# Another order for the beginning of a packed-attention and gated feed-forward kernel

## The chip, the cores and the metric

The kernel runs on one core of a Trainium2 chip. Time is device time in microseconds (us), from an execution's start to its end; the runs before have a median of 695.22 us (three runs, 694.74 to 695.33).

## The reference

`x` is the result of an attention in two steps, and a gated feed-forward layer follows it:

```python
def _attn_ref(q, k, v, p):                       # q, k, v: 8 x 8 x 576 x 64; p: 8 x 8 x 32 x 64
    p_packed = sm_attn(p, k, v)                  # softmax(p k^T / 8) v
    return sm_attn(q, p_packed, p_packed)        # softmax(q p_packed^T / 8) p_packed

def _moe_ref(x, w_in, w_out):                    # x: 4608 x 512, w_in: 512 x 2048, w_out: 2048 x 512
    h = x @ w_in
    sp = np.maximum(h, 0.0) + np.log1p(np.exp(-np.abs(h)))
    return (h * erf(sp)) @ w_out
```

The weights come as 64-bit floats, so that a row of 512 of them is 4 KB.

## The kernel before, in words

The eight batches go one after the other, batches 0 and 1 in a beginning of their own. For a batch, `attention` computes the packed queries' scores against k, their softmax, and its product with v (the packed values); then the scores of q against the packed values and a second softmax, `second_softmax`, whose result is kept in two parts, `a2h` and `a2l` (a rounded value and the rest). The feed-forward layer never forms x: `w_prime` multiplies the packed values with a piece of w_in, the result is split into `wph` and `wpl` (`w_prime_high`, `w_prime_low`), and `h_half` multiplies these with a2: six products of 288 columns for 128 rows of h. Two such halves are a unit: unit n is half a batch's tokens (288) and 256 of the 2048 columns. `h_copy` brings them from PSUM to SBUF, `softplus`, `erf` and `gate` follow, and `o_part` multiplies with w_out.

For batch 0 the second softmax is split by token halves: N is the one of the first 288 tokens, X the one of the other 288. Units 0 to 3 (first half of the tokens) need N alone, units 4 to 7 need X.

Pieces of w_in: piece 0 (columns 0 to 511) is fetched in two halves, numbered 4 and 5 (256 columns each, 256 KB per chunk of 128 rows, four chunks); piece 1 is columns 512 to 1023 (512 KB per chunk). A fetched chunk is turned to 32 bits by a cast on ScalarE (line 121) and an operation on VectorE (line 125). Units 0 and 4 use half-piece 4, units 1 and 5 half-piece 5, and units 2, 3, 6, 7 piece 1.

The order of the beginning is written out by hand: `BEGINNING` is a list of words, each word calls one part, and `keep_order` makes every engine keep it. So what stands behind a word on its engine waits for it. The words that matter here: A and B are the next step of the attention of batch 0 and of batch 1; `F4.2` fetches chunk 2 of piece 4 on the SyncE (SP) queue, `F3` w_out's block 3; L and K are its cast and its operation; `W0.1`, `G0.1` (or H) and `V0.1` are w_prime of batch 0 and piece 1, its high and its low part; `h3.0` is the first half of unit 3, c and d copy it on ScalarE and VectorE; s, e and m are softplus, erf and gate; N and X are the next step of either half; `i11` is 11 products of the identity matrix with itself, whose result nobody uses.

The steps of batch 1 (`attention(1)`): its transfers of p and k; of v; of q; first scores (two words, each with a copy to SBUF behind it, lines 385 and 349); the maximum over them (line 427); two exponentials (452); six transposes of the result (402); their copy (460); four more transposes (407), and so on. At the end of the beginning's fourth line of words, at `h4.0`, both orders meet and are the same from there.

Of the kernel before, what the change touches and what calls it, by code (L numbers as in the profile page):

```python
# [8 lines left out]
F32 = mybir.dt.float32  # L9
F32R = mybir.dt.float32r  # L10
# [3 lines left out]
F16 = mybir.dt.float16  # L14
# [11 lines left out]
EXPONENT, TINY = 0x7F800000, 2.0 ** -55  # L26

BEGINNING = """
A A F4.2 F5.2 F4.3 A F5.3 F4.1 i11 A A i8 F5.1 F4.0 F5.0 A A A A F3 F1.2 B F1.3 F1.0 F1.1 A F2 A A A A A L5.2 L4.2 A A
A A A A L4.1 F0 F5 F1 N i21 B N N X L5.1 F7 N K4.1 K5.1 N L4.0 K5.2 K4.0 L4.3 N K4.3 K4.2 W0.4 N L5.0 K5.0 L5.3 N F4  # L30
H0.4 V0.4 K5.3 L3 N X i2 i1 i2 N X L1.2 W0.5 H0.5 V0.5 K1.2 B B B B B B L1.3 h1.0 c1.0 L1.0 K1.0 K1.3 L1.1 K1.1 X h1.1
F2.0 c1.1 h0.0 d0.0 X W0.1 G0.1 V0.1 L2 h0.1 h3.0 F6 X h3.1 d0.1 X X X X B B B s1 s0 e0 L0 F2.1 h2.0 h2.1 d2.1 c3.0
h4.0 h4.1 K0 L1 B d2.0 d3.1 e1 m0 h5.0 L5 B h5.1 d4.0 B c4.1 K1 o0.0 o0.2 K2 s3 d5.1 B L4 s2 s4 e4 S0 d5.0 o0.1 m1 K3
o1.2 T0 B B K5 o1.0 e3 K4 L7 m4 B L6 m3 K7 K6 h6.0 S1 o0.3 B c6.0 S4 R6 h6.1 T1 B B B c6.1 B S3 U4 o1.3 h7.0 e2 m2
h7.1 s5 o1.1 o2.1 o3.1 e5 B R2 B B o2.3 F2.3 d7.0 v4 T3 o2.0 F2.2 c7.1 L2.2 m5 T2 B B F3.2 L2.0 p3.1 o3.3 s6 p3.3 o2.2
# [15 lines left out]
def tile_pack_attention_moe(ctx: ExitStack, tc: tile.TileContext, qT, kT, v, pT, w_in, w_out, outT):  # L51
    nc = tc.nc
    P = 128
    B, _, NC, S = qT.shape
    DFF = w_in.shape[1]
    DM = w_out.shape[1]
    HT = S // 2
# [9 lines left out]
    NK = 32  # L67
# [3 lines left out]
    NB0 = 2  # L71
# [9 lines left out]
    apool = ctx.enter_context(tc.tile_pool(name="attn", bufs=2))  # L81
# [179 lines left out]
    a2 = {}  # L261
    pt = {}
    wp = {}
    halves = {}
# [15 lines left out]
    def second_softmax(b, ta, tb, mx, hi, lo, h0, h1, at=None, high=nc.scalar.copy):  # L280

        half = hi.dtype == F16

        cols = slice(h0, h1)
        blocks = ta[:, :, cols].rearrange("p r (n k) -> p r n k", k=NK)
        mx = mx[:, :, h0 // NK:h1 // NK]
        wide = mx.unsqueeze(3).to_broadcast([P, 2, (h1 - h0) // NK, NK])
        if at is not None:
            for r in range(2):
                nc.vector.transpose(ta[:, r, cols], at[r][:, 0:HT])  # L290
            yield
        nc.vector.tensor_reduce(mx, blocks, axis=AX.X, op=ALU.max)
        yield
        nc.vector.tensor_tensor(blocks, blocks, wide, op=ALU.subtract)
        yield
        nc.scalar.activation(ta[:, :, cols], ta[:, :, cols], AF.Exp, scale=SCALE)
        yield
        nc.vector.tensor_reduce(mx, blocks, axis=AX.X, op=ALU.add)
        yield
        if half:  # L300
            nc.vector.tensor_scalar(mx, mx, 1e-9, 2.0 ** -15, op0=ALU.add, op1=ALU.mult)
        else:
            nc.vector.tensor_scalar(mx, mx, 1e-9, None, op0=ALU.add)
        nc.vector.reciprocal(mx, mx)
        yield
        nc.vector.tensor_tensor(blocks, blocks, wide, op=ALU.mult)
        yield
        if h1 - h0 == S:
            nc.vector.transpose(tb[:].rearrange("p r s -> p (r s)"), ta[:].rearrange("p r s -> p (r s)"))
        else:  # L310
            for r in range(2):
                nc.vector.transpose(tb[:, r, cols], ta[:, r, cols])
        yield
        high(hi[:, :, cols], tb[:, :, cols])
        yield
        nc.vector.tensor_tensor(lo[:, :, cols], tb[:, :, cols], hi[:, :, cols], op=ALU.subtract)
        yield

    def attention(b):

        joined, third, roomy = b > NB0, b == NB0, b == 0
# [3 lines left out]
        def chunk(name, tag="kvq"):  # L325
            if tag == "kvq":
                return apool.tile([P, S], F32, name=f"{name}_{b}", tag="kvq", bufs=6)[:]
            if tag == "wo":
                return opool.tile([P, S], F32, name=f"{name}_{b}", tag="wo")[:]
            return tpool.tile([P, S], F32, name=f"{name}_{b}", tag=tag)[:]  # L330

        def bank(name, single=False):

            if single:
                return [ps_h.tile([P, 512], F32, name=f"{name}_{b}_{x}", tag="ps_h")[:] for x in range(2)], None
            if name in at_o:
                d = at_o[name]
                return [ps_o.tile([P, 512], F32, name=f"{name}_{b}_{x}", tag=f"ps_o{d + x}")[:] for x in range(2)], None
            ps = ps_m.tile([P, 2, 512], F32, name=f"{name}_{b}", tag="ps_m")
            return [ps[:, 0, :], ps[:, 1, :]], ps  # L340
# [19 lines left out]
        q_at = ("t0", "t0", "t0", "t1") if roomy else ("wo",) * NC if b == 1 else ("kvq",) * NC  # L360
        values, q = [], []

        def load_v():
            for j in range(NCH):
                n, t0 = (CH, j * CH) if j < NT else (REM, NT * CH + (j - NT) * REM)
                values.append(chunk(f"v{j}", v_at[j]))
                nc.sync.dma_start(values[j][0:n, 0:2 * NC * 64], v[b, t0:t0 + n, :])

        def load_q():
            for c in range(NC):  # L370
                q.append(chunk(f"q{c}", q_at[c]))
                nc.sync.dma_start(q[c], qT[b, :, c, :])

        if not joined:
            load_v()
            yield
            load_q()
            yield
        a1 = apool.tile([P, 2, S], F32, name=f"a1_{b}", tag="big", bufs=3)
        scores = []  # L380
        for c2 in range(2):
            banks = bank(f"s1_{c2}", joined or (third and c2 == 1))
# [67 lines left out]
        else:  # L450
# [20 lines left out]
            if joined:  # L471
                load_q()
# [24 lines left out]
            two_over(inverse[b][:], po[:, P:2 * P])  # L497
        yield
        ta = apool.tile([P, 2, S], F32, name=f"ta{b}", tag="big", bufs=3)
        for c2 in range(2):  # L500
            banks = bank(f"s2_{c2}", b > NB0 + 1 or (b >= NB0 and c2 == 0) or (b == 1 and c2 == 1))
            for c in range(NC):
                for r in range(2):
                    nc.tensor.matmul(banks[0][r][NK * c:NK * c + NK, 0:HT], ptt[64 * r:64 * r + 64, NK * c:NK * c + NK],  # L504
                                     q[c][64 * r:64 * r + 64, c2 * HT:(c2 + 1) * HT], start=True, stop=True)
            yield
            if roomy:
                scores.append(banks[0])
            else:
                for r in range(2):  # L510
                    nc.vector.transpose(ta[:, r, c2 * HT:(c2 + 1) * HT], banks[0][r][:, 0:HT])
                yield
        tb = apool.tile([P, 2, S], F32, name=f"tb{b}", tag="big", bufs=3)
        kind = F32R if b < NB0 else F16
        hi = apool.tile([P, 2, S], kind, name=f"a2h{b}", tag="a2h")
        lo = apool.tile([P, 2, S], kind, name=f"a2l{b}", tag="a2l")
        a2[b] = (hi, lo)
        mx = apool.tile([P, 2, S // NK], F32, name=f"mx{b}", tag="mx")
        if roomy:
            halves["N"] = second_softmax(b, ta, tb, mx, hi, lo, 0, HT, scores[2])  # L520
            halves["X"] = second_softmax(b, ta, tb, mx, hi, lo, HT, S, scores[3], nc.vector.tensor_copy)
            yield
            return
        every = second_softmax(b, ta, tb, mx, hi, lo, 0, S, None, nc.vector.tensor_copy if b < NB0 else nc.scalar.copy)
        for k, _ in enumerate(every):
            yield
# [242 lines left out]
    def attend(b):  # L769
        if b not in gens:  # L770
            gens[b] = attention(b)
        next(gens[b])
# [17 lines left out]
    f = 2  # L790
# [46 lines left out]
    def fetch(*which):  # L837
# [1 line left out]

    parts = {  # L840
        "A": lambda: attend(0), "B": lambda: attend(1), "C": lambda: attend(2),
        "N": lambda: next(halves["N"]), "X": lambda: next(halves["X"]),
        "F": fetch, "L": lambda *w: fetched[w][0](), "K": lambda *w: fetched[w][1](),
        "S": split_w_out_high, "T": split_w_out_low,
        "W": w_prime, "H": w_prime_high, "V": w_prime_low,
# [54 lines left out]
```

## Time and profile before

| | |
|---|---|
| runs | 694.74, 695.33, 695.22 us (median 695.22) |
| the profiled execution | 696.22 us, its span 694.4 us |
| TensorE (PE) busy | 679.4 us, 98% of the span |
| VectorE (DVE) busy | 600.4 us, 86% |
| ScalarE (ACT) busy | 556.2 us, 80% |
| GpSimd (POOL) busy | 53.7 us, 8% |
| DMA share by fortieth of the span, tenths | 9996456358351512211122301131021101000010 |

The span is cut into 40 slices of 17.4 us; the DMA engines are full in the first two and a half. A busy time counts PE's modelled ends, so small waits of PE are to be read from the list of waits and from the start times. A timeline row gives the start and the duration from the first to the last end in us, engine, line, operation, output and input with the number of records, and in brackets the idle time before it with what ended it. A 32-bit product counts as two records on PE.

### The profile page before, as it was taken

Reading aid. Unit: us, or ns where it says so; the run is one execution under the profiler, and the core shown is the slowest. Engines: PE = TensorE matmul, PEld = TensorE weight load, DVE = VectorE, ACT = ScalarE, POOL = GpSimd, SP = SyncE. Lnnn points to the kernel's source line nnn. Section 1 sums busy time; section 2 is a strip of 40 time slices with the busy share of each in tenths; the row PEclk is TensorE's granted clock in tenths of the full one; section 3 lists DMA queues with packets and bytes.
Section 4 is the critical chain, followed back from the end, with each engine's and each line's share of the span. In section 5 each row is a group of like instructions: output and inputs, shape, how many; then the busy total and the mean of one; then the engine's idle time right before and its main releaser. Section 6 shows DMA issues by size and latency. Waiting matters only on the chain.

```text
span 694.4 us, 15628 instructions
## 1 busy us (share of the span) xinstructions
PE 679.4 (98%) x6442; PEld 538.0 (77%) x6442; DVE 600.4 (86%) x937; ACT 556.2 (80%) x981; POOL 53.7 (8%) x80
## 2 busy tenths in 40 slices
PE   8999998999999999999999999999999999999997
PEld 6687988998888777867777776777777677777775
DVE  4999998889996999889988899798988899877775
ACT  2799977877778779887888888887898878787784
POOL 2031123102451000000000000000000000000000
PEclk9999999999999999999999999999999999999999
DMA  9996456358351512211122301131021101000010
GB/s 317 402 335 216 154 170 228 105 179 256 35 93 11 138 42 92 69 53 65 35 59 87 100 1 52 39 121 66 9 82 52 36 1 35 1 9 27 2 35 34
DMA packets 34311, 66.81 MB, mean 96 GB/s; under 512 B 4032, under 2 KB 13248, under 8 KB 34240
## 3 DMA queue, kind: packets, MB, share of 16 engines
q1 hardware_dynamic: 29600, 56.31, 24.4%
q0 software_dynamic: 4352, 8.92, 5.2%
q8 instruction: 50, 0.82, 0.5%
q10 hardware_dynamic: 288, 0.59, 0.2%
q14 instruction: 21, 0.17, 0.1%
HBM read 49.81 MB, written 15.99 MB: 95 GB/s over the span
## 4 chain that ended last, share of the span: by engine, by line
PE 62%; ACT 15%; DVE 13%; DMA 5%; issue 4%; POOL 1%; SPq 0%; ACTq 0%; POOLq 0%; DVEq 0%
PE o L637 35%; PE h L585 18%; PE wp L538 3%; DVE t L670 3%; DVE t L671 3%; ACT t L668 3%; ACT t L666 3%; ACT t L673 2%; ACT u L669 2%; DMA k<-kT 2%; DMA wi<-w_in 2%; DVE gl L620 2%; ACT ob L649 2%; PE p L414 1%; PE s L504 1%
## 5 line engine op out<-in xcount | busy, mean ns | idle before, releaser
L637 PE MATMUL o<-gh,woh 128*128 128x288 f16 x1536 | 304.5, 286 | 1.8 <-ACT ob L647 0.9
L637 PEld LDWEIGHTS <-woh 128*128 128x128 f16 x2304 | 223.4, 98 | 68.3 <-issue 12.8
L637 PE MATMUL o<-gl,woh 128*128 128x288 f16 x768 | 219.6, 286 | 0.5 <-DVE gl L620 0.4
L585 PE MATMUL h<-a2h,wph 128*128 128x288 f16 (+1 forms) x512 | 149.4, 292 | 4.2 <-ACT hs L593 2.8
L585 PE MATMUL h<-a2h,wpl 128*128 128x288 f16 (+1 forms) x512 | 147.7, 289 | 0.7 <-DVE wpl L562 0.7
L585 PE MATMUL h<-a2l,wph 128*128 128x288 f16 (+1 forms) x512 | 147.5, 288 | 0.0
L670 DVE SCALAR_TENSOR_TENSOR t<-hs,gs,t 128x576 f32<-128x576 f32 x96 | 78.3, 815 | 51.6 <-ACT u L669 50.9
L620 DVE TENSOR_TENSOR gl<-hs,gh 128x576 f16<-128x576 f32 (+1 forms) x124 | 96.3, 776 | 4.8 <-ACT gh L613 0.8
L673 ACT ACTIVATE t<-t 128x576 f32<-128x576 f32 x96 | 65.8, 686 | 41.6 <-DVE t L671 39.7
L637 PE MATMUL o<-gh,wohl 128*128 128x288 f32 x448 | 97.8, 299 | 0.0
L595 ACT ACTIVATE hs<-h 128x288 f32<-128x288 f32 x192 | 71.8, 407 | 30.5 <-PE h L585 28.5
L585 PEld LDWEIGHTS <-wph 128*128 128x128 f16 x768 | 74.9, 98 | 20.8 <-issue 1.8
L637 PEld LDWEIGHTS o<-gh,wohl 128*128 128x128 f32 x448 | 74.2, 188 | 6.4 <-issue 2.7
L671 DVE SCALAR_TENSOR_TENSOR t<-u,t 128x576 f32<-128x576 f32 x96 | 72.8, 758 | 3.3
L675 DVE SCALAR_TENSOR_TENSOR hs<-t,hs 128x576 f32<-128x576 f32 x96 | 71.9, 749 | 2.4 <-ACT t L673 2.4
L666 ACT ACTIVATE t<-hs,gs 128x576 f32<-128x576 f32 x96 | 73.7, 768 | 0.0
L668 ACT ACTIVATE t<-t 128x576 f32<-128x576 f32 x96 | 65.6, 684 | 3.0
L669 ACT ACTIVATE u<-t 128x576 f32<-128x576 f32 x96 | 65.6, 683 | 3.1
L637 PE MATMUL o<-gl,wohl 128*128 128x288 f32 x224 | 66.2, 295 | 0.0
L613 DVE CAST gh<-hs 128x576 f16<-128x576 f32 (+1 forms) x117 | 55.4, 474 | 4.3 <-PE o L637 4.0
L585 PEld LDWEIGHTS <-wpl 128*128 128x128 f16 x384 | 37.6, 98 | 9.5
L637 PEld LDWEIGHTS o<-gl,wohl 128*128 128x128 f32 x224 | 42.2, 188 | 0.1
(126 smaller groups left out, 824.4 us busy)
## 6 DMA issues: line engine op xcount, KB each, us to landing
q<-qT SPq DMA_DIRECT2D x32, 288.0 KB, 4.2
k<-kT SPq DMA_DIRECT2D x30, 288.0 KB, 5.2
wos<-w_out SPq DMA_DIRECT2D x16, 512.0 KB, 6.0
outT<-ob SPq DMA_DIRECT2D x48, 144.0 KB, 1.8
v<-v SPq DMA_DIRECT2D x24, 256.0 KB, 4.2
wi<-w_in SPq DMA_DIRECT2D x12, 512.0 KB, 6.9
outT<-ob POOLq DMA_DIRECT2D x32, 144.0 KB, 3.7
scratch<-wo POOLq DMA_DIRECT2D x16, 256.0 KB, 3.3
```

The source lines that it names most:

```text
L585: nc.tensor.matmul(ps[:, 0:HT], w[:, r, fo:fo + P], a[:, r, c * HT:(c + 1) * HT], start=(m == 0), stop=(m == 5))
L595: nc.scalar.mul(dst, src, 2.0 ** -19)
L613: copy(ghi[:], gs[n][0][:])
L620: nc.vector.tensor_tensor(glo[:], hs[:], ghi[:], op=ALU.subtract)
L637: nc.tensor.matmul(acc[b, c, d][:, 0:HT], w[f][:, d * P:(d + 1) * P], gg[:, k, :], start=(first and k == 0 and m == 0), stop=(last and k = ...
L666: nc.scalar.activation(t[:], hs[:], AF.Tanh, bias=T_BIAS, scale=scale[:, 0:1])
L668: nc.scalar.activation(t[:], t[:], AF.Square, bias=root * Q_BIAS, scale=root * Q_SCALE)
L669: nc.scalar.activation(u[:], t[:], AF.Tanh, bias=U_BIAS, scale=U_SCALE / A2)
L670: nc.vector.scalar_tensor_tensor(t[:], hs[:], scale[:, 1:2], t[:], op0=ALU.mult, op1=ALU.add)
L671: nc.vector.scalar_tensor_tensor(t[:], u[:], A1, t[:], op0=ALU.mult, op1=ALU.add)
L673: nc.scalar.activation(t[:], t[:], AF.Tanh, bias=A_BIAS, scale=A_SCALE)
L675: nc.vector.scalar_tensor_tensor(hs[:], t[:], 1.0, hs[:], op0=ALU.add, op1=ALU.mult)
```

## The change

The list of words is written anew up to `h4.0`, and two functions are cut so that it can be. (1) q of batch 0 is fetched in two column blocks per chunk (144 KB each instead of 288 KB), the second behind all of half-piece 5 (word Q). (2) The scores of its first block and N come first; the second block's scores are a step of their own behind `W0.4`. (3) Half-piece 4 is fetched before half-piece 5, and unit 0 is computed before unit 1. (4) Piece 1 of w_in is fetched before batch 1's p and k and before w_out's block 3. (5) Batch 1's first scores go behind units 0 and 1 on PE, and its maximum behind `V0.1` on VectorE. (6) Identity products: 11, 8, 13, 9, 3 and 6 instead of 11, 8, 21, 2, 1 and 2.

One line of the table, before and now:

```diff
-H0.4 V0.4 K5.3 L3 N X i2 i1 i2 N X L1.2 W0.5 H0.5 V0.5 K1.2 B B B B B B L1.3 h1.0 c1.0 L1.0 K1.0 K1.3 L1.1 K1.1 X h1.1
+K5.3 N h0.0 c0.0 h0.1 L1.3 c0.1 F4 K5.1 K5.0 W0.5 X X K1.2 H0.5 L1.0 V0.5 K1.3 L1.1 K1.0 B h1.0 c1.0 h1.1 c1.1 B B B B K1.1 X i3 W0.1
```

```diff
-        def load_q():
+        def load_q(c2=None):
             for c in range(NC):
-                q.append(chunk(f"q{c}", q_at[c]))
-                nc.sync.dma_start(q[c], qT[b, :, c, :])
+                if not c2:
+                    q.append(chunk(f"q{c}", q_at[c]))
+                cols = slice(0, S) if c2 is None else slice(c2 * HT, (c2 + 1) * HT)
+                nc.sync.dma_start(q[c][:, cols], qT[b, :, c, cols])
 
         if not joined:
             load_v()
             yield
-            load_q()
+            load_q(0 if roomy else None)
+            halves["Q"] = lambda: load_q(1)
             yield
...
-        for c2 in range(2):
+
+        def scores_of(c2):
             banks = bank(f"s2_{c2}", b > NB0 + 1 or (b >= NB0 and c2 == 0) or (b == 1 and c2 == 1))
...
+        if roomy:
+            near = scores_of(0)
+            tb = apool.tile([P, 2, S], F32, name=f"tb{b}", tag="big", bufs=3)
+            mx = results()
+            halves["N"] = second_softmax(b, ta, tb, mx, *a2[b], 0, HT, near)
+            yield
+            far = scores_of(1)
+            halves["X"] = second_softmax(b, ta, tb, mx, *a2[b], HT, S, far, nc.vector.tensor_copy)
+            yield
+            return
```

VectorE around batch 1's maximum (output `m`, from `a_1`, the copied scores), before: `wpl_4` is the low part of half-piece 5, the rows of `w_in_sb` are piece 1, `mx` and `ta` are X, `wph_1` and `wpl_1` are `G0.1` and `V0.1`.

```order
L294 TENSOR_TENSOR ta_282<-ta_282,mx_306 128x2x288
L562 TENSOR_TENSOR wpl_4_384<-wp_5_401,wph_4_383 128x2x256
L125 SCALAR_TENSOR_TENSOR w_in_sb<-wi_2_204,w_in_sb 128x512
L427 TENSOR_REDUCE m_446<-a_1_421 128x2
L428 TENSOR_SCALAR m_446<-m_446 128x2
L125 SCALAR_TENSOR_TENSOR w_in_sb<-wi_0_218,w_in_sb 128x512
L125 SCALAR_TENSOR_TENSOR w_in_sb<-wi_3_216,w_in_sb 128x512
L125 SCALAR_TENSOR_TENSOR w_in_sb<-wi_1_220,w_in_sb 128x512
L593 COPY hs_0_0_477<-h_0_0_0_478 128x288
L298 TENSOR_REDUCE mx_306<-ta_282 128x2x9
L555 CAST wph_1_496<-wp_1_487 128x1024
L562 TENSOR_TENSOR wpl_1_497<-wp_1_487,wph_1_496 128x1024
```

The same place now:

```order
L574 TENSOR_TENSOR wpl_4_354<-wp_5_412,wph_4_353 128x2x256
L125 SCALAR_TENSOR_TENSOR w_in_sb<-wi_3_208,w_in_sb 128x512
L125 SCALAR_TENSOR_TENSOR w_in_sb<-wi_0_210,w_in_sb 128x512
L125 SCALAR_TENSOR_TENSOR w_in_sb<-wi_1_212,w_in_sb 128x512
L294 TENSOR_TENSOR ta_288<-ta_288,mx_302 128x2x288
L567 CAST wph_1_498<-wp_1_486 128x1024
L574 TENSOR_TENSOR wpl_1_499<-wp_1_486,wph_1_498 128x1024
L298 TENSOR_REDUCE mx_302<-ta_288 128x2x9
L430 TENSOR_REDUCE m_523<-a_1_456 128x2
L431 TENSOR_SCALAR m_523<-m_523 128x2
```

The maximum stood ahead of piece 1's last three chunks, and now stands behind the low part of piece 1's result and one step of X.

PE around `W0.1` (output `wp_1`), before, from the identity products to batch 1's first scores (outputs `s`, from k of batch 1):

```order
L833 MATMUL idle<-ident 128x128 x21
L538 MATMUL wp_4_366<-w_in_sb,pt_280 32x256 x8
L833 MATMUL idle<-ident 128x128 x5
L538 MATMUL wp_5_401<-w_in_sb,pt_280 32x256 x8
L385 MATMUL s_0_1_0_422<-k_1_208,p_206 32x288
```

And now, from the end of batch 1's first scores to unit 3 (output `h_0_3`):

```order
L388 MATMUL s_1_1_0_469<-k_1_219,p_214 32x288
L388 MATMUL s_1_1_1_470<-k_1_219,p_214 32x288
L845 MATMUL idle<-ident 128x128 x3
L550 MATMUL wp_1_486<-w_in_sb,pt_284 32x512 x8
L845 MATMUL idle<-ident 128x128 x6
L597 MATMUL h_0_3_0_512<-a2h_300,wph_1_498 128x288
```

The 16 score products stood right behind `W0.5`, ahead of all of h; now all of units 0 and 1 stands ahead of them, and `W0.1` waits behind them.

ScalarE around batch 1's exponentials (output `a_1`), before:

```order
L349 COPY a_1_421<-s_1_1_1_435 128x288
L121 CAST w_in_sb<-wi_3_216 128x512
L593 COPY hs_0_1_452<-h_0_1_0_453 128x288
L121 CAST w_in_sb<-wi_0_218 128x512
L121 CAST w_in_sb<-wi_1_220 128x512
L296 ACTIVATE ta_282<-ta_282 128x2x288
L593 COPY hs_0_1_452<-h_0_1_1_467 128x288
L121 CAST wo_500<-wos_224 128x512
L452 ACTIVATE a_1_421,sm_447<-a_1_421,m_446 128x576 x2
L600 ACT_TABLE_LOAD
L600 ACTIVATE t_0_1_544<-hs_0_1_452 128x576
L600 ACTIVATE t_0_0_546<-hs_0_0_477 128x576
```

And now:

```order
L349 COPY a_1_456<-s_1_1_1_470 128x288
L296 ACTIVATE ta_288<-ta_288 128x2x288
L121 CAST wo_508<-wos_226 128x512
L121 CAST wo_520<-wos_228 128x512
L455 ACTIVATE a_1_456,sm_524<-a_1_456,m_523 128x576 x2
L612 ACT_TABLE_LOAD
L612 ACTIVATE t_0_1_553<-hs_0_1_439 128x576
L612 ACTIVATE t_0_0_555<-hs_0_0_390 128x576
L615 ACT_TABLE_LOAD
L615 ACTIVATE t_0_0_555<-t_0_0_555 128x576
L121 CAST wo_558<-wos_317 128x512
L605 COPY hs_0_3_511<-h_0_3_0_512 128x288
```

The casts and copies between the copied scores and the exponentials went ahead of the scores; from the exponentials on (table load, softplus, erf, and behind them the copy of batch 1's transposes) the order is the one of before.

## Rows read from the trace of the kernel before

**Rows 1.** Busy time by engine (number of records), clock and DMA, in one stretch.

```profile
25.00:30.00 5.00, 4.78 (x63) 3.05 (x63) 4.93 (x8) 4.24 (x10) 0.53 (x1) 1.00 1.03 409
```

**Rows 2.** Chain of work that ended last, start and duration, 19 to 37 us.

```profile
19.60 6.93 DMA k<-kT
...
30.89 1.30 DVE w_in_sb L125 x2
...
32.23 1.14 PE wp L538 x12
...
33.40 1.23 DVE wph L555
...
34.65 1.23 DVE wpl L562
...
35.93 1.60 PE h L585 x10
```

**Rows 3.** Timeline of DVE, 16 to 30 us.

```profile
16.61 0.85 DVE L290 STREAM_TRANSPOSE ta<-s 128x288 f32<-128x288 f32 x2 [2.43 <-PE s L504]
17.49 0.75 DVE L292 TENSOR_REDUCE mx<-ta 128x18 f32<-128x576 f32 x1
...
21.89 0.27 DVE L304 RECIPROCAL mx<-mx 128x18 f32<-128x18 f32 x1
...
22.68 0.75 DVE L306 TENSOR_TENSOR ta<-ta,mx 128x576 f32<-128x576 f32 x1
...
23.68 0.83 DVE L312 STREAM_TRANSPOSE tb<-ta 128x288 f32<-128x288 f32 x2
24.44 0.65 DVE L562 TENSOR_TENSOR wpl<-wp,wph 128x512 fp32r<-128x512 f32 x1
...
28.68 1.35 DVE L427 TENSOR_REDUCE m<-a 128x2 f32<-128x1152 f32 x1
```

**Rows 4.** Timeline of ACT, 24 to 42 us.

```profile
24.65 0.66 ACT L314 CAST a2h<-tb 128x576 fp32r<-128x576 f32 x1
...
26.22 0.59 ACT L555 CAST wph<-wp 128x512 fp32r<-128x512 f32 x1 [0.23 <-PE wp L538]
...
29.15 0.43 ACT L593 COPY hs<-h 128x288 f32<-128x288 f32 x1
...
30.41 0.78 ACT L121 CAST w_in_sb<-wi 128x512 f16<-128x512 bf16 x1 [0.16 <-DMA wi<-w_in]
...
32.55 0.77 ACT L452 ACTIVATE a<-a,m 128x576 f32<-128x576 f32 x1
...
34.18 1.28 ACT L600 ACT_TABLE_LOAD   x1
...
36.60 0.69 ACT L600 ACTIVATE t<-hs 128x576 f32<-128x576 f32 x1 [0.45 <-DVE hs L593]
...
40.76 0.80 ACT L460 COPY a1t<-t 128x768 f32<-128x768 f32 x1
```

**Rows 5.** Timeline of PE, 1 to 54 us.

```profile
1.39 5.06 PE L833 MATMUL idle<-ident 128*128 128x128 f32 x22 [1.39 <-POOL ident masks.py:199]
...
14.91 2.15 PE L504 MATMUL s<-q,pt 64*32 64x288 f32 x32 [0.35 <-ACT pt L493]
16.99 4.96 PE L833 MATMUL idle<-ident 128*128 128x128 f32 x42
...
25.14 0.83 PE L538 MATMUL wp<-w_in_sb,pt 64*32 64x256 f32 x14 [0.38 <-DVE wpl L562]
...
37.37 0.82 PE L402 MATMUL t<-ident,a 128*128 128x128 f32 x6
...
42.01 0.60 PE L407 MATMUL p<-ident,a 128*96 128x128 f32 x4
...
52.30 1.42 PE L504 MATMUL s<-q,pt 64*32 64x288 f32 x32
```

**Rows 6.** What PE waited for, 80 to 300 us: total, times, longest.

```profile
PE h L585 <- ACT hs L593: 2.8, 4, 1.2
```

More of the change, by code (lines that the diff above doesn't have):

```diff
@@ L28 @@
 BEGINNING = """
-A A F4.2 F5.2 F4.3 A F5.3 F4.1 i11 A A i8 F5.1 F4.0 F5.0 A A A A F3 F1.2 B F1.3 F1.0 F1.1 A F2 A A A A A L5.2 L4.2 A A
-A A A A L4.1 F0 F5 F1 N i21 B N N X L5.1 F7 N K4.1 K5.1 N L4.0 K5.2 K4.0 L4.3 N K4.3 K4.2 W0.4 N L5.0 K5.0 L5.3 N F4
-H0.4 V0.4 K5.3 L3 N X i2 i1 i2 N X L1.2 W0.5 H0.5 V0.5 K1.2 B B B B B B L1.3 h1.0 c1.0 L1.0 K1.0 K1.3 L1.1 K1.1 X h1.1
-F2.0 c1.1 h0.0 d0.0 X W0.1 G0.1 V0.1 L2 h0.1 h3.0 F6 X h3.1 d0.1 X X X X B B B s1 s0 e0 L0 F2.1 h2.0 h2.1 d2.1 c3.0
+A A F4.2 F4.3 A F4.1 F4.0 i11 A A i8 F5.2 F5.3 F5.1 F5.0 A A A A Q F1.2 F1.3 F1.0 F1.1 B A F3 F2 A A A A A L4.2 L4.3 A A
+A K4.2 K4.3 A i13 L4.1 F0 F5 F1 N N N L4.0 L5.2 N K4.1 K4.0 W0.4 A L5.3 N H0.4 N N V0.4 i9 B L5.1 L5.0 N K5.2 F7 N L1.2
+K5.3 N h0.0 c0.0 h0.1 L1.3 c0.1 F4 K5.1 K5.0 W0.5 X X K1.2 H0.5 L1.0 V0.5 K1.3 L1.1 K1.0 B h1.0 c1.0 h1.1 c1.1 B B B B K1.1 X i3 W0.1
+X F2.0 G0.1 V0.1 i6 L3 h3.0 X L2 B F6 X h3.1 X X X X B B B s1 s0 e0 L0 F2.1 h2.0 h2.1 d2.1 c3.0
 h4.0 h4.1 K0 L1 B d2.0 d3.1 e1 m0 h5.0 L5 B h5.1 d4.0 B c4.1 K1 o0.0 o0.2 K2 s3 d5.1 B L4 s2 s4 e4 S0 d5.0 o0.1 m1 K3
@@ L505, in attention, with results @@
                                      q[c][64 * r:64 * r + 64, c2 * HT:(c2 + 1) * HT], start=True, stop=True)
-            yield
[L507 to L521, printed above, removed]
+            return banks[0]
+        def results():
+            kind = F32R if b < NB0 else F16
+            a2[b] = [apool.tile([P, 2, S], kind, name=f"a2{x}{b}", tag=f"a2{x}") for x in "hl"]
+            return apool.tile([P, 2, S // NK], F32, name=f"mx{b}", tag="mx")
+        if roomy:
[3 more added lines that the diff above has]
+            halves["N"] = second_softmax(b, ta, tb, mx, *a2[b], 0, HT, near)
+            yield
+            far = scores_of(1)
+            halves["X"] = second_softmax(b, ta, tb, mx, *a2[b], HT, S, far, nc.vector.tensor_copy)
             yield
             return
+        for c2 in range(2):
+            banks = scores_of(c2)
+            yield
+            for r in range(2):
+                nc.vector.transpose(ta[:, r, c2 * HT:(c2 + 1) * HT], banks[r][:, 0:HT])
+            yield
+        tb = apool.tile([P, 2, S], F32, name=f"tb{b}", tag="big", bufs=3)
+        mx = results()
+        hi, lo = a2[b]
         every = second_softmax(b, ta, tb, mx, hi, lo, 0, S, None, nc.vector.tensor_copy if b < NB0 else nc.scalar.copy)
@@ L841, in tile_pack_attention_moe @@
         "A": lambda: attend(0), "B": lambda: attend(1), "C": lambda: attend(2),
-        "N": lambda: next(halves["N"]), "X": lambda: next(halves["X"]),
+        "Q": lambda: halves["Q"](), "N": lambda: next(halves["N"]), "X": lambda: next(halves["X"]),
         "F": fetch, "L": lambda *w: fetched[w][0](), "K": lambda *w: fetched[w][1](),
```

## The prediction

> **What bounds the kernel now.** I read the busy times first: PE works for 679.4 of 694.4 us. So a change of the first 40 us gains only what it takes out of PE's waits and identity products there, and loses every wait that it puts before the common part; later work shifts as a block. Next I read the beginning's chain of waits. It runs over arriving data: batch 1's k is in at 26.53 [rows 2], the last chunk of w_in's piece 1 at 30.4, where ScalarE waits for it [rows 4]. The DMA engines are full then, 409 GB/s [rows 1]. From there the chain is dense: last chunk ready at 32.2, `W0.1` until 33.4, its high and low parts 1.23 us each, and unit 3's products run on from 35.93 [rows 2]. Third, ScalarE's timeline, for what stands behind: batch 1's exponentials end at 34.18, then come a table load, softplus, a second table, erf, casts, and at 40.76 to 41.56 the copy of batch 1's transposes [rows 4]. PE asks for that copy at 42.01 [rows 5]: it is ready 0.45 us before. This slack is what the change will eat.
>
> **The change, part by part.** I walk the new order down the engines with durations of the old rows.
>
> *Data.* Ahead of piece 1's last chunk p, k of batch 1 and one w_out block go away: 1.24 + 0.52 = 1.77 MB, at 409 GB/s 4.3 us, so it is in at 26.1 instead of 30.4. Batch 1's k now comes behind three more 512 KB chunks and ahead of one such block: 1.05 MB net, 2.6 us, so it is in at 29.1 instead of 26.53. The half blocks of q carry the same bytes.
>
> *N and unit 0.* The old scores of q began at 14.91 and took both halves [rows 5]; eight products take about half of the 1.42 us that 16 take later [rows 5], so the first transposes start no sooner than 15.6 and at the latest at 16.61 as before [rows 3]; I take 15.9, because the old products still waited for q. Then on VectorE and ScalarE: transposes 0.85, maximum 0.75, subtraction 0.75 (the multiplication's row), exponential 0.66 (the cast's row, same shape), sum 0.75, addition and reciprocal 0.45, multiplication 0.75, `V0.4` 0.65 and transposes 0.83 [rows 3, 4]: 6.45 us, to 22.35. Cast 0.66: 23.0. Low part 0.75: 23.8. Identity products (13 and 9, each 0.24 us by 42 records in 4.96 us [rows 5]) lie in PE's waits beside this and cost nothing as long as they end first: nine behind the second scores end at 22.9. Six products of h take 0.86 (10 of them lie between 35.93 and 37.37 [rows 2, 5]). So `h0.0` ends at 24.7; its copy (0.43 [rows 4]) must free the PSUM bank for `h0.1`, since the identity products hold the other: 25.2 to 26.0.
>
> *`W0.5` and unit 1.* `W0.5` started at 25.14 before and its high part at 26.22 [rows 4, 5], 1.08 later: now 26.0 and 27.1. High part 0.59, low part 0.65 behind it: 28.4. `h1.0` ends at 29.2, copy, `h1.1` until 30.5. Here unit 0 and unit 1 are done; before, unit 0's second half lay beside `G0.1`. That is the gain, and it is spent at once:
>
> *Batch 1's scores and `W0.1`.* The 16 products, 1.35, end at 31.9 (k has been in since 29.1: hidden). Three identity products, 0.7: `W0.1` starts at 32.6. Before, 12 of its 16 records took from 32.23 to 33.40; whole it takes 1.4: 34.0. `G0.1` and `V0.1`, 1.25 each with the handover: 36.5. Unit 3 runs on from 36.5, **0.6 later** than 35.93. So the piece that arrives 4.3 us earlier is used later, because on PE it stands behind batch 1's scores, and these behind unit 1. VectorE has nothing to do from about 30.2 to 34.0.
>
> *Batch 1's maximum.* It now waits behind `V0.1` and a sum of X: 36.5 + 0.67 = 37.15; it takes 1.35 [rows 3] and its scaling 0.2: 38.65, where the maximum alone was started at 28.68 before. ScalarE then does the exponentials, 32.55 to 34.18 before, 38.7 to 40.3 now; it is idle from about 35. PE's six transposes start at 39.5 and end at 40.75 instead of 37.37 to 37.94: PE has been done with unit 3 since 37.9, and `h2.0` comes **2.8 later**.
>
> *The copy behind them.* From the exponentials' end to that copy's end ScalarE took 34.18 to 41.56, 7.4 us, 0.45 of it a wait for a copy by VectorE [rows 4] that is long done now. I take 6.8: the copy is ready at 47.1. PE, 4.07 us of products behind `h2.0`, stands there at 44.8 and waits until 47.1. Before, it went on at 42.01: **5.1 later**. From here nothing is in another order, each engine is shifted alike, and PE has no slack to give back. The sum: 694.4 + 5.1 = 699.5 for the span, 696.22 + 5.1 = 701.3 for the profiled execution; that one is 1.0 above the median, so against the median 695.22 + 5.1 = **700.3 us**, slower by 0.7%.
>
> *Bounds.* The loss can't be less than what k's arrival leaves: 29.1 + 1.35 + 0.7 puts `W0.1` at 31.2, 1.4 earlier than walked: +3.7, 698.9. Upwards, no row shows blocks of half the size; if each of the eight costs as much as a whole one (0.72 us), k comes 2.9 later, at 32.0, and the scores 1.4 later: +6.5, 701.7. Below nothing is excluded, bytes are bytes. I keep 0, the near end, since queue and row count stay. The DMA issues that are added (four on SP) lie in a queue that waits for the engines anyway.
>
> **A rule against it: the clock.** Before, the first 22 identity records take 0.230 us each, 42 later ones 0.118 [rows 5]: half speed (1.2 GHz) and full (2.4 GHz), and after the first stretch PE never stands idle as long again; the longest wait later is 1.2 us [rows 6]. The change makes waits of some 1.6 and 2.3 us. The Trainium skill ("TensorE: Matmul & The Clock Gate", Part 1) says that the array falls back to half speed after it has been idle for a while and needs sustained work to return. No run here shows yet how this program takes it; it is the third rival.
>
> **Rivals.**
>
> *Faster: the second piece follows its data.* Were `W0.1` to start soon after 26.1 and the old 5.5 us from arrival to unit 3 held, the whole beginning would move by 4.3: 690.9. The point from which it decides: exponentials end 7.7 us behind `W0.1`'s start, and the copy 6.8 after that; to meet 42.01, `W0.1` must start before 27.5. For it: the arrival. Against it: k, 1.6 us behind that point even by arrival, and unit 1 ahead of k. Chance 0.03.
>
> *Absorbed.* Between 80 and 300 us PE waits 2.8 us in all for ScalarE's copies of h [rows 6]. If what ends these waits has its own pace (transfers through GpSimd's queue), PE arrives late and finds it done: 700.3 - 2.8 = 697.5. For it: VectorE and ScalarE are not fuller than before. Against: these copies stand behind casts whose buffers are freed by work that follows PE itself. Chance 0.12.
>
> *The clock falls* during the two waits. Price by the one stretch at half speed that the trace has, 5.06 us long [rows 5]: half of it lost, 2.5 us: 702.8. Against: between the two waits PE works for 4 us. Chance 0.10.
>
> **How the numbers follow.** The walk has 0.73, with its own range 698.9 to 701.7; the rest of 0.02 is for what I don't see. The range takes in absorption and clock: 697.4 to 703.1. A measurement of this kernel can tell about 0.2%, 1.4 us. Faster by more (under 693.8): 0.03. Within (up to 696.6), by full absorption of a loss at its lower bound: 0.05. Slower: 0.92.
>
> **What would show it.** After: units 0 and 1 done by 31 us; `W0.1` near 32.6 with its chunks long ready; VectorE idle before `G0.1`; batch 1's maximum near 37 instead of 28.7; ScalarE idle ahead of the exponentials; PE waiting for them at its transposes, and again for the copy near 47. Wrong: the maximum before 32, `W0.1` before 28, or a start of the common part that is late while the end is not.

## The result and the profile after

The changed kernel takes 702.48 us (median of five runs, 701.89 to 702.86) where the kernel before takes 695.22: a ratio of 1.0098, 95% interval 1.0084 to 1.0111. The forecast was 700.3, range 697.4 to 703.1. The profiled execution took 701.89 us, its span is 700.1 us. PE is busy for 681.7 us of it, 97%.

First VectorE's timeline of the changed kernel. The columns are those of [rows 3]; every line number of a function behind the edit has moved by 3 to 12.

```profile
15.59 0.85 DVE L290 STREAM_TRANSPOSE ta<-s 128x288 f32<-128x288 f32 x2 [0.90 <-PE s L508]
...
28.57 1.89 DVE L125 SCALAR_TENSOR_TENSOR w_in_sb<-wi,w_in_sb 128x512 uint32<-128x512 uint32 x3
...
34.18 1.23 DVE L567 CAST wph<-wp 128x1024 fp32r<-128x1024 f32 x1 [3.06 <-PE wp L550]
35.44 1.22 DVE L574 TENSOR_TENSOR wpl<-wp,wph 128x1024 fp32r<-128x1024 f32 x1
36.58 0.74 DVE L298 TENSOR_REDUCE mx<-ta 128x18 f32<-128x576 f32 x1
37.24 1.34 DVE L430 TENSOR_REDUCE m<-a 128x2 f32<-128x1152 f32 x1
```

The first softmax half starts 1.0 us earlier than in [rows 3]. Piece 1's last chunks are turned by 30.46, in [rows 2] by 32.2. Then VectorE stands idle for 3.06 us: `wp` is not there. Batch 1's maximum (L430), at 28.68 in [rows 3], runs at 37.24, behind both parts of `wp` and a sum of X.

PE's timeline of the same execution says why `wp` is late, and what the late maximum costs:

```profile
20.40 1.67 PE L508 MATMUL s<-q,pt 64*32 64x288 f32 x16 [0.90 <-DMA q<-qT]
...
22.00 2.27 PE L845 MATMUL idle<-ident 128*128 128x128 f32 x18
24.04 0.38 PE L597 MATMUL h<-a2h,wph 128*128 128x288 f32 x1
...
26.57 0.66 PE L550 MATMUL wp<-w_in_sb,pt 64*32 64x256 f32 x16
...
30.99 1.20 PE L388 MATMUL s<-k,p 64*32 64x288 f32 x32
32.12 0.94 PE L845 MATMUL idle<-ident 128*128 128x128 f32 x6
32.98 1.09 PE L550 MATMUL wp<-w_in_sb,pt 64*32 64x512 f32 x16
...
39.81 0.55 PE L405 MATMUL t<-ident,a 128*128 128x128 f32 x3 [1.49 <-ACT a L455]
...
42.61 0.44 PE L597 MATMUL h<-a2h,wph 128*128 128x288 f32 x1
...
47.41 0.64 PE L410 MATMUL p<-ident,a 128*96 128x128 f32 x4 [0.80 <-ACT a1t L463]
...
57.75 1.77 PE L508 MATMUL s<-q,pt 64*32 64x288 f32 x32
```

Units 0 and 1 and batch 1's scores (30.99) stand ahead of `W0.1` (32.98), whose data had been ready for 2.5 us. The transposes wait 1.49 us for the exponentials; the second group of transposes, L407 at 42.01 in [rows 5], comes at 47.41, after a wait for the copy on ScalarE.

ScalarE's timeline, the lines that answer to [rows 4]:

```profile
22.20 0.68 ACT L314 CAST a2h<-tb 128x576 fp32r<-128x576 f32 x1 [1.29 <-DVE tb L312]
...
38.88 0.78 ACT L455 ACTIVATE a<-a,m 128x576 f32<-128x576 f32 x1 [3.69 <-DVE mx L303]
...
40.53 1.28 ACT L612 ACT_TABLE_LOAD   x1
...
46.55 0.80 ACT L463 COPY a1t<-t 128x768 f32<-128x768 f32 x1
```

ScalarE is idle for 3.69 us ahead of the exponentials (the releaser named, `mx`, is X's scaling, right behind that of `m`). The copy ends at 47.35, where [rows 4] had 41.56. That ScalarE chain, 40.5 to 47.35, is 6.8 us long, as the walk took it.

One thing more, in the windows of the changed kernel:

```profile
40.00:45.00 5.00, 4.79 (x26) 4.55 (x26) 2.51 (x5) 4.94 (x8) 0.00 (x0) 0.66 1.03 346
```

The granted clock (column behind POOL) is 0.66 in this stretch: from 41.55 on it was half for 3.4 us, behind the 1.49 us wait. The products of h, 0.133 us apart at full speed, are 0.24 apart there. PE still waits 0.80 us for the copy.

### The profile page after: what moved, and what is told of

It is laid out like the page before. It is cut to its first block, busy times and chain, and to the rows that moved or that the text cites. A ratio compares the mean times of both kernels' runs of the same rounds, so it can differ in the third digit from the quotient of the medians.

```text
span 700.1 us, 15663 instructions
## 1 busy us (share of the span) xinstructions
PE 681.7 (97%) x6452; PEld 540.5 (77%) x6452; DVE 600.4 (86%) x935; ACT 558.8 (80%) x983; POOL 53.8 (8%) x80
## 4 chain that ended last, share of the span: by engine, by line
PE 50%; DVE 21%; ACT 17%; DMA 7%; issue 3%; POOL 1%; SPq 0%; ACTq 0%; POOLq 0%; DVEq 0%
PE o L649 29%; PE h L597 15%; DVE t L682 5%; DVE t L683 4%; DVE gl L632 3%; ACT t L680 3%; ACT t L678 3%; PE wp L550 3%; DMA wos<-w_out 2%; ACT u L681 2%; ACT t L685 2%; DMA wi<-w_in 2%; DVE hs L687 2%; ACT ob L661 2%; DVE gh L625 1%
## 5 line engine op out<-in xcount | busy, mean ns | idle before, releaser
L682 DVE SCALAR_TENSOR_TENSOR t<-hs,gs,t 128x576 f32<-128x576 f32 x96 | 78.3, 816 | 51.8 <-ACT u L681 51.3
```

What stands on the lines that cost most here:

```text
L682: nc.vector.scalar_tensor_tensor(t[:], hs[:], scale[:, 1:2], t[:], op0=ALU.mult, op1=ALU.add)
```

## The experiments

The twelve runs were made in four groups, each beside runs of the kernel before on the same chip (medians 694.97, 694.74, 695.31 and 694.90 us). "Above before" is a median less that of its group. "Queue theory" is the walk: the maximum, late on VectorE, and PE's order behind it set the loss.

**e0_before**, the kernel before, unedited.

> The kernel before, once more, for a second trace of it. All theories: 695.2 us, the copy of batch 1's transposes ends near 41.6 and the four transposes behind it start near 42.0. It is to tell why the two profiled executions lie 5.7 us apart (spans 694.4 and 700.1) and the medians 7.3: if the first trace was 1 us above its kernel's usual time, this one's span lies near 693.4.

694.67 us, ratio 0.9997 (0.9985 to 1.0009), span 693.0. That is 1.4 us less span than the first trace of it. PE's starts in the two traces differ by up to 0.7 us in the first 30 us, agree within 0.03 us from `W0.1` (31.1) until 119.7 us, and differ by 1.4 from 122 us on. The place is shown under e12_after.

**e1_max_early**, the maximum alone put back.

```diff
-... h1.1 c1.1 B B B B K1.1 X i3 W0.1
-X F2.0 G0.1 V0.1 i6 L3 h3.0 X L2 B F6 ...
+... h1.1 c1.1 B B B B K1.1 X B i3 W0.1
+X F2.0 G0.1 V0.1 i6 L3 h3.0 X L2 F6 ...
```

> The changed kernel, with batch 1's maximum ahead of piece 1's high part on VectorE instead of behind its low part. Theory queue (the maximum stands behind the low part, so the exponentials, a table load and the copy of the transposes come late): the copied scores are there at 33.2, the maximum ends at 34.6, the exponentials run behind two casts from 35.2 to 36.9 instead of 38.9 to 40.5, the copy ends near 43.7 instead of 47.4, no stretch at half clock; 702.5 - 3.7 = 698.8 us. Theory data (batch 1's k and the halves of q come late): no change, 702.5. Theory clock (the stretch at half speed from 41.5 to 44.9 is the price): that stretch goes with PE's waits, 702.5 - 1.7 = 700.8.

698.28 us, ratio 1.0047 (1.0032 to 1.0062), 3.3 above before: the queue theory's number within 0.5. VectorE, ScalarE and PE of this kernel:

```profile
34.42 1.35 DVE L430 TENSOR_REDUCE m<-a 128x2 f32<-128x1152 f32 x1 [2.08 <-ACT a L349]
```

```profile
36.08 0.79 ACT L455 ACTIVATE a<-a,m 128x576 f32<-128x576 f32 x1
...
43.76 0.79 ACT L463 COPY a1t<-t 128x768 f32<-128x768 f32 x1
```

```profile
44.88 0.60 PE L410 MATMUL p<-ident,a 128*96 128x128 f32 x4
```

Exponentials and copy come 2.8 us earlier than in the changed kernel, and PE no longer waits for the copy; it is itself 2.9 us late at 44.88. Of these, 1.2 us belong to this execution, one of the longer of its six runs: its `W0.1` starts at 34.19, the one of the changed kernel's first trace at 32.98. So the maximum's place is worth about half; the rest is PE's own lateness, and a wait of 1.22 us near 124 us that is taken up under e12_after.

**e2_before_max_late**, the reverse: the kernel before, with only the maximum moved behind `V0.1`.

```diff
-... K1.2 B B B B B B L1.3 ...   W0.1 G0.1 V0.1 L2 h0.1 ...
+... K1.2 B B B B B L1.3 ...   W0.1 G0.1 V0.1 B L2 h0.1 ...
```

> The kernel before, with one thing changed: batch 1's maximum behind the low part of piece 1 on VectorE. Theory queue: the maximum runs from 35.9 to 37.2 instead of 28.7 to 30.1, the exponentials from 37.4 to 39.0, the copy ends at 45.9 instead of 41.6, PE is 3.9 late behind it: 699.1 us. Theories data and clock: 695.2, since transfers, units and identity products stay (the clock alone could fall in a wait of about 3 us).

699.74 us, ratio 1.0071 (1.0055 to 1.0087): 4.8 above before, without any other part of the change. PE of this kernel:

```profile
40.48 0.55 PE L402 MATMUL t<-ident,a 128*128 128x128 f32 x3 [0.82 <-ACT a L452]
...
48.03 0.77 PE L407 MATMUL p<-ident,a 128*96 128x128 f32 x4 [2.27 <-ACT a1t L460]
```

The same two waits as in the changed kernel, made by one moved word. The profiled execution is the longest of its runs (span 700.6): its `W0.1` began 2.1 us later than in the first trace of before (33.24 against 31.12, behind a wait of 1.60 us for q), and behind the second wait its clock was half from 48.4 to 51.8.

**e4_no_i3**, the changed kernel without the three identity products ahead of `W0.1`.

```diff
-... K1.1 X i3 W0.1
+... K1.1 X W0.1
```

> The changed kernel without the three identity products ahead of piece 1's product on PE. Theory queue counts them on the path, since PE has its data then: everything from there is 0.8 earlier, 701.7 us. Theory that identity products lie in waits and are free: 702.5.

701.08 us, ratio 1.0086 (1.0073 to 1.0099), 6.1 above before, 1.2 less than the changed kernel and 1.0 less than its repetition (e12_after): the three were on the path (walked: 0.7). The traces alone don't show it: `W0.1` starts at 32.34 and PE's second group of transposes at 46.82, both 0.6 earlier than in the first trace of the changed kernel but at most 0.14 earlier than in e12_after. Here the second scores of q began at 19.15 instead of 20.40 and 19.91, and the clock was half from 29.1 to 32.5, during batch 1's scores.

**e3_warm**, six identity products more, into a spare PSUM tile, where PE waits for the exponentials.

```diff
+    def warm(n):
+        spare = ps_m.tile([P, 2, 512], F32, name="spare", tag="ps_m")
+        for _ in range(n):
+            nc.tensor.matmul(spare[:, 0, 0:P], ident[:], ident[:], start=True, stop=True)
-... X h3.1 X X X X B B B s1 ...
+... X h3.1 J6 X X X X B B B s1 ...
```

> The changed kernel with six more identity products behind unit 3, ahead of batch 1's transposes, where PE stands 1.5 us waiting for the exponentials. The clock fell to half for 3.4 us right behind that wait. Queue theory: PE meets the late copy of batch 1's transposes anyway, so the clock costs nothing: 702.5, within 0.5. Clock theory: the half-speed stretch is part of the loss; kept at work PE does not fall, and the products of h behind it end 1.7 us earlier: 700.8.

700.75 us, ratio 1.0090 (1.0076 to 1.0104), 6.0 above before. The time is the clock theory's, the trace is not:

```profile
47.56 1.07 PE L410 MATMUL p<-ident,a 128*96 128x128 f32 x4 [2.27 <-ACT a1t L463]
```

The clock did not fall at 41.6, PE was at the copy 1.3 us earlier, and waited 2.27 instead of 0.80 us. Behind this longer wait the clock was half from 47.6 to 51.0. This was the longest of its four runs (702.20), and no trace shows the others. Their mean granted clock is on record: 1.000 and 0.999 in the two short ones (700.00 and 700.26), 0.997 in the other two (701.25 and 702.20). What the six products gained is taken up under e12_after.

**e5_k_first**, the old fetch order at this place.

```diff
-Q F1.2 F1.3 F1.0 F1.1 B A F3 F2
+Q F3 F1.2 B F1.3 F1.0 F1.1 A F2
```

> The changed kernel with the old fetch order of this place: w_out's block 3, then piece 1's chunks with batch 1's p and k between the first and the second. Queue theory: an earlier k is of no use, since batch 1's scores stand behind unit 1 on PE; piece 1's last chunk, late again (30.4 instead of 26.1), holds up casts in front of unit 1's copies on ScalarE, so it gets worse: near 704.5. Data theory (batch 1's k arrives too late in the changed kernel, and that makes the scores and all behind them late): faster, near 700.

706.86 us, ratio 1.0183 (1.0159 to 1.0207), 12.1 above before: the queue theory's sign, 2.4 above its size. ScalarE and PE of this kernel:

```profile
28.85 0.77 ACT L121 CAST w_in_sb<-wi 128x512 f16<-128x512 bf16 x1 [3.97 <-DMA wi<-w_in]
```

```profile
30.41 0.61 PE L597 MATMUL h<-a2h,wph 128*128 128x288 f32 x1 [3.81 <-ACT wph L567]
```

A cast of piece 1 waits 3.97 us for its chunk, and unit 1's high part waits behind it in ScalarE's queue; then the clock was half for 6.8 us. So the new order of words needs the early piece 1: not for `W0.1`, but because its casts stand in front of unit 1. An earlier k gave nothing.

**e6_w_first**, `W0.1` ahead of batch 1's scores, no `i3`.

```diff
-... c1.1 B B B B K1.1 X i3 W0.1
+... c1.1 K1.1 X W0.1 B B B B
```

> The changed kernel with piece 1's w_prime on PE ahead of batch 1's scores instead of behind them, and without the three identity products there; the maximum stays behind the low part. Queue theory: high and low part start 1.9 us earlier and the maximum, exponentials and copy with them: 700.6. Data theory (something that arrives sets the start of w_prime): no change, 702.5.

699.81 us, ratio 1.0082 (1.0069 to 1.0096), 5.1 above before. PE of this kernel:

```profile
30.25 1.09 PE L550 MATMUL wp<-w_in_sb,pt 64*32 64x512 f32 x16
...
44.73 0.64 PE L410 MATMUL p<-ident,a 128*96 128x128 f32 x4 [0.78 <-ACT a1t L463]
```

`W0.1` starts 2.7 us earlier and the copy follows by 2.7 (0.9 of it because q's second blocks came earlier in this execution: unit 0 starts at 23.11). No arrival holds `W0.1`, the order on PE does.

**e8_no_fill**, without the identity products from the low part of half-piece 4 on.

```diff
-... N N V0.4 i9 B ...   K1.1 X i3 W0.1   ... V0.1 i6 L3 ...
+... N N V0.4 B ...   K1.1 X W0.1   ... V0.1 L3 ...
```

> The changed kernel without the identity products from the low part of half-piece 4 on (9, 3 and 6). My step that they cost nothing: 702.5. Queue theory as the changed kernel's trace now shows it (nine of them end later than the cast of a2 and stand ahead of unit 0, and they hold the PSUM bank that the second half of h needs): the beginning moves 1.5 to 2.1 us forward, 700.4 to 701.0. Clock theory: without them PE falls to half speed before unit 0 and loses what it gained: 702.5 or more.

699.11 us, ratio 1.0070 (1.0058 to 1.0083), 4.4 above before and so 2.9 less than the changed kernel, where the queue theory had 1.5 to 2.1. In its trace the loading of k for batch 1's scores waits 0.61 us, until 29.39: here the beginning has come forward to k's arrival, which the walk had at 29.1. In both traces of the changed kernel nothing waits for k.

**e10_no_i9**, only the nine left out.

```diff
-... N N V0.4 i9 B ...
+... N N V0.4 B ...
```

> The changed kernel without the nine identity products behind the low part of half-piece 4 alone (the three and the six stay). If these nine are what e8_no_fill got its gain from (they end 1.0 us behind the cast of a2 and hold the PSUM bank that the second half of unit 0 needs): about 1.9 us earlier, 700.6. My own step, that they cost nothing: 702.5.

704.39 us, ratio 1.0135 (1.0122 to 1.0148), 9.1 above before: a miss, worse than the changed kernel by 2. The starts of unit 0 on PE, and the granted clock by windows, in e8_no_fill and then in e10_no_i9:

```profile
22.24 0.40 PE L597 MATMUL h<-a2h,wph 128*128 128x288 f32 x1 [1.22 <-ACT a2h L314]
23.03 0.40 PE L597 MATMUL h<-a2l,wph 128*128 128x288 f32 x1 [0.40 <-DVE a2l L316]
...
24.69 0.66 PE L550 MATMUL wp<-w_in_sb,pt 64*32 64x256 f32 x16
```

```profile
25.00:30.00 5.00, 3.98 (x64) 2.39 (x56) 3.95 (x7) 3.03 (x7) 1.05 (x2) 1.00 1.02 400
```

```profile
22.75 0.40 PE L597 MATMUL h<-a2h,wph 128*128 128x288 f32 x1 [1.42 <-ACT a2h L314]
23.55 0.61 PE L597 MATMUL h<-a2l,wph 128*128 128x288 f32 x1 [0.40 <-DVE a2l L316]
```

```profile
25.00:30.00 5.00, 3.77 (x26) 2.27 (x25) 2.14 (x4) 2.93 (x6) 0.00 (x0) 0.50 1.02 380
30.00:35.00 5.00, 4.51 (x43) 3.01 (x42) 2.34 (x4) 1.40 (x4) 1.05 (x2) 0.50 1.03 408
```

Without the nine, unit 0 starts 1.3 to 1.8 us earlier (0.2 and 0.7 of it because `W0.4` came earlier in these executions), and in e8_no_fill `W0.5` follows at 24.69 instead of 26.57. But PE then waits 1.2 to 1.4 us for `a2h` and 0.4 for `a2l`. In e10_no_i9 the clock was half from 23.6 to 37.2, which takes everything back and more; in e8_no_fill it fell only at 35. Up to batch 1's scores both have the same program, so what decides between them stays open; e8_no_fill ran on another chip than e10_no_i9 and e9_early_no_fill, and no run separates that. By the mean granted clocks on record it is no matter of the one traced execution: 0.994 to 0.995 in all five runs of e8_no_fill, 0.987 to 0.992 in all four of e10_no_i9. The nine products ended late by about 1.2 us, but in every trace that has them the clock stayed up until 29 us at least; of the three without, it fell before 25 in two.

**e9_early_no_fill**, e1_max_early and e8_no_fill together.

```diff
-... N N V0.4 i9 B ...   K1.1 X i3 W0.1   ... V0.1 i6 L3 h3.0 X L2 B F6 ...
+... N N V0.4 B ...   K1.1 X B W0.1   ... V0.1 L3 h3.0 X L2 F6 ...
```

> The changed kernel with both repairs together: batch 1's maximum ahead of piece 1's high part (as in e1_max_early), and no identity products from the low part of half-piece 4 on (as in e8_no_fill). Queue theory: the two act on the same chain one behind the other and add, 2.9 and 3.0 us of their traces' 5.8 at 50 us, as far as PE's own work allows; PE's fourth transposes then stand where they stood before the change: 695.5, within 1. If a third cause is left (arrival of batch 1's k, or the clock), it ends above 697.

697.61 us, ratio 1.0038 (1.0026 to 1.0051), 2.3 above before: the third cause that the expectation left room for. PE has no wait at the second group of transposes, but the granted clock is half in the stretch ahead of it:

```profile
35.00:40.00 5.00, 4.49 (x18) 4.16 (x19) 4.76 (x10) 4.94 (x7) 0.00 (x0) 0.50 1.06 279
```

Here PE is the bound, so half speed costs time: it lasted from 34.4 to 41.2 us and began in a wait of 3.0 for the high part, with nothing left to fill it. How much of the 2.3 us this is stays open: the two of the twelve runs with the highest mean clock (0.998) are the shortest (695.84 and 696.12), but runs at 0.995 took 696.39 to 700.40.

**e11_scores_first**, meant to beat both kernels.

```diff
-Q F1.2 F1.3 F1.0 F1.1 B A F3 F2
+Q F1.2 F1.3 B F1.0 F1.1 A F3 F2
-... K5.0 W0.5 X X K1.2 H0.5 L1.0 V0.5 K1.3 L1.1 K1.0 B h1.0 c1.0 h1.1 c1.1 B B B B K1.1 X i3 W0.1
-X F2.0 G0.1 V0.1 i6 L3 h3.0 X L2 B F6 X h3.1 X X X X B B B s1 ...
+... K5.0 W0.5 B B X X K1.2 H0.5 B B B L1.0 V0.5 K1.3 B h1.0 c1.0 L1.1 K1.0 h1.1 c1.1 B B K1.1 X X L3 W0.1
+F2.0 G0.1 V0.1 h3.0 X L2 F6 X h3.1 X X X X B s1 ...
```

> A version meant to be better than both: as changed, but batch 1's p and k are fetched between piece 1's second and third chunk, its scores stand right behind half-piece 5's product on PE, its maximum ahead of piece 1's, and the three and six identity products are gone. Queue theory: the fourth transposes start where they did before the change, since PE itself is then the bound there: 695, within 0.7, no gain over before. If the earlier piece 1 were worth anything by itself: under 693.8.

697.19 us, ratio 1.0026 (1.0015 to 1.0038): the best variant of the changed kernel, and still 1.9 above before; the 695 of the queue theory is missed by 2.2.

```profile
32.50 1.59 PE L550 MATMUL wp<-w_in_sb,pt 64*32 64x512 f32 x16 [1.46 <-DVE w_in_sb L125]
...
43.19 0.60 PE L410 MATMUL p<-ident,a 128*96 128x128 f32 x4
```

Now `W0.1` does wait for its last chunk, 1.46 us, because k was let in front of it, and PE has no wait at the second transposes: it is the bound there, 1.2 us later than before. The nine identity products are still in this kernel.

**e12_after**, the changed kernel, unedited.

> The changed kernel once more, unedited. Queue theory: the copy of batch 1's transposes ends near 47.3 again and PE waits for it, whether or not the clock falls, so PE's fourth transposes stand 5.0 to 5.9 us behind those of before. What comes on top of that in the first trace (0.4 near 53 us, 1.1 near 120 us) I take for a matter of the single execution: it should come out otherwise here, between 0 and 2. Time 701.4 to 702.8. If six products against the clock (e3_warm, 6.0 above its before where the changed kernel was 7.3) really gained, this run must be 7 or more above its before; if it is near 6, they gained nothing.

702.01 us (701.31 to 702.11), ratio 1.0097 (1.0084 to 1.0111), 7.1 above before. PE of this run:

```profile
46.86 0.64 PE L410 MATMUL p<-ident,a 128*96 128x128 f32 x4 [2.29 <-ACT a1t L463]
...
126.79 0.40 PE L597 MATMUL h<-a2h,wph 128*128 128x288 f32 x1 [1.41 <-ACT hs L605]
```

Its granted clock was 1.00 in every window from 5 to 690 us, and PE waited 2.29 us at the copy, where the first trace waited 0.80 with a clock that had fallen. So the half-speed stretch of the changed kernel costs nothing there. The ten runs of the changed kernel agree: by their mean granted clock two had no such stretch (1.000: 701.55 and 702.56 us), and the eight at 0.995 to 0.998 took 701.31 to 702.86.

But the mark set for e3_warm came out the other way: this run is 7.1 above its before, so the six products did gain about 1 us (6.0 above). They did not gain it ahead of the copy, which in e3_warm's trace PE takes up at 47.56, later than here. In that trace the clock fell behind the copy, where PE no longer waits, and the runs at 1.000 and 0.999 are the short ones. Why these are shorter than the changed kernel's two runs at 1.000 no run shows; four runs are few, and the cause stays open.

The second row is most of the rest of the loss. Its cause, GpSimd's timeline, in e0_before, in the first trace of before, in the changed kernel, and here:

```profile
118.10 0.53 POOL L152 MEMSET wo<- 128x512 f32 x1 [2.12 <-DMA scratch<-wo]
```

```profile
119.59 0.52 POOL L152 MEMSET wo<- 128x512 f32 x1 [3.62 <-DMA scratch<-wo]
```

```profile
125.11 0.53 POOL L152 MEMSET wo<- 128x512 f32 x1 [3.26 <-DMA scratch<-wo]
```

```profile
125.16 0.52 POOL L152 MEMSET wo<- 128x512 f32 x1 [3.88 <-DMA scratch<-wo]
```

A memset of a w_out tile waits for a transfer out of that tile; ScalarE's cast into the tile waits for the memset, the copies of h stand behind the cast, and PE behind those. With 2.12 us PE does not wait at all; with 3.26 to 3.88 it waits 0.8 to 1.4. The products of h concerned, in e0_before, in the first trace of before and in the first of the changed kernel:

```profile
119.89 0.30 PE L585 MATMUL h<-a2h,wph 128*128 128x288 f32 x1
```

```profile
121.22 0.40 PE L585 MATMUL h<-a2h,wph 128*128 128x288 f32 x1 [1.18 <-ACT hs L593]
```

```profile
126.75 0.40 PE L597 MATMUL h<-a2h,wph 128*128 128x288 f32 x1 [0.80 <-ACT hs L605]
```

The other traces agree: in eight of all fourteen the memset waits 3.2 to 4.2 us and PE 0.8 to 1.7 behind it; in six (e0_before, e2_before_max_late, e3_warm, e9_early_no_fill, e10_no_i9, e11_scores_first) it waits 2.1 to 2.75 us and PE 0.3 us or not at all. So this wait is no property of the changed order alone.

## Why the prediction was right, and what it missed

**Bound, direction, mechanism: right.** PE stands where the walk put it. Both traces of the changed kernel, the walk and the kernel before (starts on their engines, us):

| | before | walk | first trace | e12_after |
|---|---|---|---|---|
| N's transposes | 16.61 | 15.9 | 15.59 | 15.11 |
| `W0.5` | 25.14 | 26.0 | 26.57 | 26.08 |
| `W0.1` | 32.23 (12 of 16) | 32.6 | 32.98 | 32.48 |
| batch 1's maximum | 28.68 | 37.15 | 37.24 | 36.74 |
| exponentials | 32.55 | 38.7 | 38.88 | 38.38 |
| PE at the second transposes | 42.01 | 47.1 | 47.41 | 46.86 |

The loss there, walked as 5.1, measured 5.4 and 4.9. The edits agree: moving the maximum back takes the loss from 7.3 to 3.3 us, moving it alone in the old kernel costs 4.8, and `W0.1`'s start is set by PE's order (e6_w_first), not by data.

That the number fits as well is in part luck. The measured 702.48 (702.01 in e12_after) lies above the walk's own range, 698.9 to 701.7, and inside the forecast's only because that was drawn up to 703.1 for the clock, which cost nothing at the place where this rival put it.

**Identity products that "cost nothing as long as they end first": the condition failed.** They were to end at 22.9 and held unit 0 until 24.04, 1.16 behind the cast of `a2h` (22.88). I had priced q's second blocks as "the same bytes", but word Q put them behind half-piece 5, and the scores waited 0.90 us for them. N began 0.3 and 0.8 us earlier than walked, so `W0.5` came only 0.6 and 0.1 us later than walked. And leaving the nine out alone (e10_no_i9) cost 2 us, in a trace with 13.7 us at half speed, while leaving out the three and the six with them (e8_no_fill) gained 2.9: their price had to be set against that of the clock.

**"From here nothing is in another order, each engine is shifted alike": the term that was mis-sized.** It carried 0 and was 1.5 in the first trace and 2.1 in e12_after: against e0_before the shift grows from 5.4 and 4.9 at the copy to 5.8 and 5.3 behind batch 1's q scores (1.77 us in the changed kernel, 1.42 in [rows 5]), and to 7.0 in both traces behind the wait at 120 us. That last wait is in [rows 6] too (the longest, 1.2): the profiled execution of before had it, and stood 1.0 above the median. The walk added its 5.1 to the median; that the median execution of before goes without this wait is likely (e0_before, 694.82 us, has none) but not shown. Added to the profiled execution it gave 701.3, and that of the changed kernel took 701.89.

**Rivals.** *Absorbed* read the waits of [rows 6] as time that a late PE could win back; against e0_before the largest of them came on top instead. *The clock falls* has nearly the measured number (702.8) for another reason: the clock fell in one trace of two and, by the mean clocks, in eight of ten runs, and the times are the same. It cost nothing where PE waited for the copy anyway, and did where PE was the bound (e9_early_no_fill, e10_no_i9). It fell in nine of the fourteen traces, behind waits of 1.4 to 3.8 us, and in e4_no_i3 at 29.1 behind waits of at most 0.74. The Trainium skill ("TensorE: Matmul & The Clock Gate", Part 1) states that a PE which stands idle falls to half speed; the traces agree. *Faster* is out: `W0.1` began at 32.98 and 32.48, not soon after 26.1, and with k, the maximum and the three and six identity products put right, e11_scores_first is still slower than before.

**Open:** why the GpSimd wait at 120 us differs between executions (2.12 and 3.62 us in two of the same kernel) and was long in both of the changed kernel; what decides whether the clock falls behind the same code; and what the six products of e3_warm gained.

## What to carry to other kernels

Data that arrives earlier was worth nothing by itself here: ask what stands ahead of its consumer on the engine, and follow every small operation that is put behind a late one (here a maximum of 1.35 us) to the next place where the bounding engine asks for it. Filler products on PE have two prices, the one for ending late and the one for the clock, and only a run of each says which is larger. Before a sum is made against a median, look whether the profiled execution shows a wait that the median doesn't have.

## What the runs showed of the hardware that was not expected

- The granted clock went to half behind waits shorter than 2 us: 1.49 us ahead of 41.55 in the changed kernel, 1.42 and 0.40 ahead of 23.6 in e10_no_i9, and only 0.74, 0.20 and 0.49 ahead of 29.1 in e4_no_i3; the changed kernel has the same three waits in both its traces, and its clock stayed up there. The stretches at half speed lasted 3.4 to 13.7 us while PE worked in them.
- The column of the granted clock reads 1.00 from 0 to 5 us in the trace of before, where the identity records are 0.230 us apart against 0.118 later. There the spacing shows the speed, and the column does not.
- A fetch of a few small blocks put last in a full queue was felt at once, and not alike in each execution: 0.90 us of PE at 20.40 in the changed kernel, 0.24 to 0.94 in the other traces with word Q, and none in e11_scores_first.
